# Identity products and moved weight work in the opening of a delta-rule attention and PReLU kernel

## The chip, the cores and the metric

One Trainium2 chip, one of its cores. The core has TensorE (PE: products; its weight loads are listed as PEld and run beside the products), VectorE (DVE), ScalarE (ACT), GpSimd (POOL) and SyncE (SP, which here issues nearly all DMAs). Each engine works its own queue in order. The metric is the device time of one execution in microseconds (us); lower is better. The kernel before takes 647.66 us, the median of three runs (646.80 to 648.08).

## The reference

Four batches, eight heads, 768 tokens, head dimension 48. The delta rule runs over the tokens of each head and reads each output before its own update; the outputs then go through a feed-forward layer with a PReLU whose slope `alpha` is one number per hidden unit:

```python
def _attn_ref(q, k, v, beta):
    k_n = k / (np.linalg.norm(k, axis=-1, keepdims=True) + 1e-06)
    state = np.zeros((B, H, D, D))
    for t in range(S):
        y[:, :, t] = q[:, :, t] @ state            # per batch and head
        v_old = state.T @ kt
        state = state + bt * outer(kt, vt - v_old)

def _moe_ref(x, w_in, w_out, alpha):               # x: (3072, 384)
    h = x @ w_in                                   # (384, 2048)
    g = np.maximum(h, 0.0) + alpha * np.minimum(h, 0.0)
    return g @ w_out                               # (2048, 384)
```

All data are 32-bit floats.

## The kernel before

**Tiling.** The tokens are cut into 12 chunks of 64; two batches share the 128 partitions, so there are 24 steps, numbered n, two for each chunk. Within a chunk the recurrence is a triangular system. It is solved by elimination on DVE and by small products on TensorE (48 or 64 rows, 64 columns, 32 for a step); a state per head is carried from chunk to chunk. The outputs are flipped and fed to the feed-forward products, which fill TensorE for most of the time. The engines' orders are written out by hand (`manual_schedule`): each engine works the instructions in the order of the program text, and waits only where data or a buffer make it.

**The opening** (L1691 to L1788) prepares steps 0 to 3 before the first state exists. For key n, `flipped` (L436) turns the tile on TensorE by four transposes (L430) and gives back ACT's copy out of PSUM (L439) as a piece, run by `now`. `grams` (L476) multiplies the flipped keys with themselves (32 products, L486). `squared` and `norms` make the keys' norms on ACT and DVE, `pick` and `picks` (L637, L647) gather the diagonal blocks of a gram, on ACT (L641) and DVE (L643), and `betas` (L325) flips the betas on TensorE (L330) and gives back four pieces, two on DVE and two on ACT (L338, L340), named `signs` where it is called. `first_weights` (L604) makes the weights from norms and betas on POOL. With all four grams gathered, `weigh_own` (L651) and `eliminate_small` (L666, called at L1782) solve the small blocks on DVE, and `first_chunk` (L1583, called at L1788) goes on from there: `place_small` makes the inverses on DVE (L706), `matrix` multiplies with them on TensorE (L857) and has ACT copy the product (L884), `own_values` does the same for the values with a copy on DVE (L895), `turn_values` follows on POOL (L873), and three rounds of products (L857, L912) lead to the outputs of the first chunk (L930). `query_flip` (L1553) and `queries` (L1562) do for the queries what `flipped` and `grams` do for the keys; the query products are copied by ACT (L1573).

**Fillers.** `identities` (L1549) multiplies the identity with itself; each call of `matmul` in 32-bit floats makes two products in the trace, so `identities(5)` is ten (L1551), written to the first bank of the second PSUM pair. `busy(n, p)` (L1534) multiplies the identity with `k_early[2]`: whole numbers of n make 512 columns, the rest a part of them (L1539). None of their results is read.

**Buffers.** Keys come through three tiles, `k_early[n % 3]` (L129), except key 3. Later keys take the places of earlier ones: key 6 goes to `k_early[0]`, key 5 to `k_early[2]`, key 4 to `k_early[1]`. The PSUM pairs `big[0]`, `big[1]`, `big[2]` hold the grams of steps 0, 1 (and 3), 2 in the opening.

**Weights.** `w_in` is fetched in pieces of 512 KB by `fetch_in(n)`, which issues DMAs on SP until n pieces are asked for. A piece is converted by two operations on ACT (`begin_in(n)`: L240, L242 for each piece, until n pieces are begun) and then by DVE (L256) and POOL (L263), called `convert` in `first_chunk`. In the opening, `fetch_in(1)` stands between the loads of keys 6 and 5 and that of key 4; the queries of steps 2 and 3 are loaded after that, then `fetch_in(STAGED)` brings the count to four. `pause` (L1666) has POOL write one element of a stage (L1668), so that SP's next weight loads wait for POOL's place in the order.

Of the kernel before, what the change touches and what calls it, by code (L numbers as in the profile page):

```python
# [43 lines left out]
def kernel(  # L44
# [11 lines left out]
    nc = tc.nc  # L56
# [17 lines left out]
    doubles, big, ffn_banks = ExitStack(), [], []  # L74
# [6 lines left out]
    def ps_one():  # L81
        return ps_big()[:, 0]
# [21 lines left out]
    def half(i):  # L104
        return slice(64 * i, 64 * i + 64)

    def dims(i):
        return slice(64 * i, 64 * i + D)
# [15 lines left out]
    ident = const.tile([128, 128], FP32, name="ident")  # L124
# [4 lines left out]
    def early(n):  # L129

        return k_late[1] if n == NKE else k_early[n % NKE]

    def fetch(a, n, dst, queues=(nc.sync, nc.sync)):
        c, bp = steps[n]
        for t in range(2):
            src = a[2 * bp + t, :, c * C : (c + 1) * C, :].rearrange("h p d -> p h d")
            queues[t].dma_start(out=dst[half(t)], in_=src)

    def load_early(n, *queues):
        if n < N:  # L140
            fetch(k, n, early(n)[:, :, 0:D], *queues)
# [15 lines left out]
    def load_q(n):  # L157
        if n < N:
            fetch(q, n, q_pad[n % NQ][:, :, 0:D])

    def load_v(n):
        if n < N:
            v_raw[n] = work.tile([128, H, D], FP32, name="v_raw", bufs=3)
            fetch(v, n, v_raw[n])
# [160 lines left out]
    def betas(first, last, p):  # L325
        n = last - first
        p = p[:, 0 : n * B * H].rearrange("p (c b t h) -> p c b t h", c=n, b=NB, t=2)
        for c in range(n):
            at = (first + c) * 128
            nc.tensor.transpose(  # L330
                p[:, c].rearrange("p b t h -> p (b t h)"), beta_sb[:, at : at + 128],
                ident[: B * H, : B * H],
            )
        to = beta_t.rearrange("p (c i) b h -> p i c b h", i=2)[:, :, first:last]

        def turned_sign(t, i):
            if i == 0 and first == 0:
                nc.vector.tensor_scalar_mul(to[half(t), i], p[half(i), :, :, t], -1.0)  # L338
            else:
                nc.scalar.mul(to[half(t), i], p[half(i), :, :, t], -1.0)  # L340

        return [lambda t=t, i=i: turned_sign(t, i) for t in range(2) for i in range(2)]
# [4 lines left out]
    def slopes():  # L347
        p = ffn_banks[1][:, 0:FT]
        nc.tensor.transpose(p, al_sb, ident[:FT, :FT])
        nc.scalar.activation(al_t, p, ACT.Copy, scale=-1.0, bias=1.0)  # L350
# [33 lines left out]
    def squared(n):  # L384
        ksq[n] = work.tile([128, H, D], FP32, name="ksq", bufs=2)
        nc.scalar.square(ksq[n], early(n)[:, :, 0:D])

    def norms(n):
        if n < 4:
            norm = first_norm[:, n]  # L390
        else:
            norm = stats[n] = work.tile([128, H], FP32, name="norm", bufs=EARLY + 3)
        nc.vector.tensor_reduce(out=norm, in_=ksq.pop(n), axis=AXX, op=ALU.add)
# [34 lines left out]
    def flip(src, p):  # L428
        for g in range(G):
            nc.tensor.transpose(  # L430
                p[0:ROWS, g * 128 : (g + 1) * 128],
                src[:, 2 * g : 2 * g + 2].rearrange("p h d -> p (h d)")[:, 0:ROWS],
                ident,
            )

    def flipped(n, p):  # L436
        flip(early(n), p)
        k_t[n] = work.tile([128, G, 128], FP32, name="k_t", bufs=EARLY + 1)
        return [lambda: nc.scalar.copy(k_t[n].rearrange("p g i -> p (g i)")[0:ROWS], p[0:ROWS])]  # L439
# [23 lines left out]
    def quarters():  # L463
        return [(g, a, t) for g in range(G) for a in range(2) for t in range(2)]

    def now(pieces):
        for x in pieces:
            x()
# [197 lines left out]
    def eliminate_small():  # L666

        flat = first_block[:, 0:512]

        def blocks_of(x):  # L670
            return x.rearrange("p (s b c) -> p c s b", s=2, c=LB)

        half_turns(
            flat.rearrange("p (s c r) -> p c s r", s=2, c=LB), blocks_of(first_flat[:, 0:512])
        )
        x = flat.rearrange("p (s r c) -> p s r c", s=2, c=LB)
        for j in range(1, LB - 1):
            n = LB - 1 - j
            prod = work.tile([128, HB * HB // 4], FP32, name="prod", bufs=2)
            prod = prod[:, 0 : 2 * j * n].rearrange("p (s c i) -> p s c i", s=2, c=j)  # L680
            nc.vector.tensor_tensor(
                out=prod,
                in0=x[:, :, 0:j, j : j + 1].to_broadcast([128, 2, j, n]),
                in1=x[:, :, j : j + 1, j + 1 : LB].to_broadcast([128, 2, j, n]),
                op=ALU.mult,
            )
            nc.vector.tensor_tensor(
                out=x[:, :, 0:j, j + 1 : LB], in0=x[:, :, 0:j, j + 1 : LB], in1=prod, op=ALU.add
            )
        nc.vector.memset(flat.rearrange("p (s e) -> p s e", s=2)[:, :, :: LB + 1], 1.0)  # L690
        own = work.tile([128, NJ * H, HB], FP32, name="inverse", bufs=1)
        own = own.rearrange("p b c -> p (b c)")[:, 0:512]
        half_turns(blocks_of(own), flat.rearrange("p (s c r) -> p r s c", s=2, c=LB))
        inverse[0] = own.rearrange("p (b c) -> p b c", c=LB)
# [155 lines left out]
    def heads(x):  # L850
        return x.rearrange("p (a g) i -> p a g i", a=2)
# [682 lines left out]
    def busy(n, p=None):  # L1534

        p = ps_one() if p is None else p
        while n > 0:
            x = p[:, 0 : int(512 * min(n, 1))]
            nc.tensor.matmul(  # L1539
                x, ident, k_early[2].rearrange("p h d -> p (h d)")[:, 0 : x.shape[-1]]  # L1540
            )
            n -= 1
# [3 lines left out]
        for _ in range(n):  # L1546
            nc.tensor.matmul(p[0:32, 0:32], ident[0:32, 0:32], ident[0:32, 0:32])

    def identities(n):  # L1549
        for _ in range(n):  # L1550
            nc.tensor.matmul(big[1][:, 0, 0:128], ident, ident)  # L1551

    def query_flip(n, p):  # L1553

        flip(q_pad[n % NQ], p)
        q_t[n] = beside[steps[n][1]][:, :, :, D : D + C]
        return lambda: nc.scalar.copy(
            q_t[n].rearrange("p t g i -> p g t i")[0:ROWS],
            p.rearrange("p (g t i) -> p g t i", g=G, t=2)[0:ROWS],
        )  # L1560

    def queries(p):  # L1562

        p = p.rearrange("p a (n g i) -> p a n g i", n=2, g=G)
        for n in range(2):
            for g, a, t in quarters():
                nc.tensor.matmul(
                    p[half(t ^ a), a, n, g], k_t[n][dims(a), g, half(t)],
                    q_t[n][dims(a), t, g],
                )  # L1570
            a_t[n] = work.tile([128, H, C], FP32, name="a_t")
        for n in range(2):
            nc.scalar.copy(heads(a_t[n]), p[:, :, n])  # L1573

        def mask(n):
            nc.gpsimd.tensor_tensor(
                out=a_t[n], in0=a_t[n], in1=minus[:, None, :].to_broadcast([128, H, C]),
                op=ALU.mult,
            )

        return mask
# [70 lines left out]
    n = 2 * W_IN_P  # L1652
# [9 lines left out]
    fetch_in, begin_in, conv_in = weights(pieces, stages, ids, in_done, STAGED, len(pieces))  # L1662
# [36 lines left out]
    def key(n):  # L1699
        return flipped(n, ffn_banks[n % 2])  # L1700

    def gram(n):
        return grams(n, big[n % 3 or n // 3], n // 3)

    identities(5)
    for n in (0, 2, 3):
        copy_late(n)
    squared(0)
    copy_0 = key(0)
    signs = betas(0, 1, big[2][:, 0])  # L1710
    norms(0)
    now(copy_0)
    now(signs)
    gram_0 = gram(0)
    squared(1)
    copy_1 = key(1)
    norms(1)
    pick(0, gram_0, 0)
# [7 lines left out]
    norms(2)  # L1726
    for n in (6, 5):
        load_early(n)
    fetch_in(1)
    now(copy_2)  # L1730
    gram_1 = gram(1)
    pick(1, gram_1, 0)
# [23 lines left out]
    turned_q = query_flip(0, ffn_banks[1])  # L1756
    load_q(2)
    turned_q()
    turned_q = query_flip(1, ffn_banks[0])
    load_q(3)  # L1760
    fetch_in(STAGED)
# [4 lines left out]
    nc.scalar.mul(minus, minus, -1.0)  # L1766
    for n in (2, 3):
        load_v(n)
    mask = queries(big[0])
    slopes()  # L1770
    for n, p in ((5, ffn_banks[0]), (6, big[2][:, 0])):
        now(flipped(n, p))
    busy(3.6, big[1][:, 0])
    copy_4 = flipped(4, big[2][:, 1])
    now(copy_4)
    begin_in(1)
    busy(1.0, big[1][:, 0])
    for n in (2, 3):
        query_flip(n, ffn_banks[3 - n])()
    begin_in(2)  # L1780
    busy(1.3, big[1][:, 0])
    eliminate_small()  # L1782

    def convert(n):
# [116 lines left out]
    n = WHOLE + PIECES - BEGUN - SOON  # L1901
# [28 lines left out]
    n = OUT_PARTS - few - 2 * rest + 1  # L1930
# [131 lines left out]
```

## Time and profile before

| what | before |
|---|---|
| median of three runs | 647.66 us (646.80 to 648.08) |
| the profiled execution's own time | 648.86 us |
| its span, first to last instruction | 647.1 us |
| mean granted TensorE clock | 0.995 |
| PE busy | 632.3 us, 98% of the span |
| DVE, ACT, POOL busy | 483.2, 259.4, 126.4 us |
| moved by DMA | 36.89 MB, mean 57 GB/s |

The span is what the profiler saw of the program; the execution's own time is 1.76 us longer. The page cuts the span into 40 slices of 16.2 us and gives busy shares in tenths (9 is 90% or more); PEclk is the granted TensorE clock:

```profile
PE   7889999999999999999999999999999999999997
PEld 6567787567889989989989989989999999999997
DVE  5868689978998788578678577678868568477383
ACT  6678555245553253254154144034045054042240
POOL 7188510010001000000000010000044053062360
PEclk9799999999999999999999999999999999999999
```

The first three slices hold TensorE below 90%, and the second has the only clock under 0.9. The stages at issue all lie in the first 42 us. In the other views a line reads: start, length, engine, line of the kernel, operation, what is written and from what, shapes and how many; in brackets how long the engine was idle before it, and what ended that idle time. A matmul's length includes the way through the array, so products that follow each other overlap in the list.

### The profile page before, as it was taken

The page shows a single profiled execution, that of the slowest core. Times are in us where ns is not written, and L with a number is a line of the kernel's source. Part 1 is how long each engine was busy: PE and PEld are TensorE (multiplying, and loading weights), DVE is VectorE, ACT ScalarE, POOL GpSimd, SP SyncE. Part 2 cuts the span into 40 slices and gives each one's busy share as a digit, 9 for nine tenths or more (in the row PEclk, how much of TensorE's full clock was granted, in tenths as well). Part 3 has the DMA queues.
Part 4 walks back from the last instruction along what each step waited for, and adds up shares of the span by engine and source line. Part 5 has one row for each costly group of instructions (what it writes and reads, how often), then busy time and mean ns, then how long its engine had stood idle before and what let it go on. Part 6 is the DMA issues. An engine that isn't in the chain of part 4 may idle for free.

```text
span 647.1 us, 21355 instructions
## 1 busy us (share of the span) xinstructions
PE 632.3 (98%) x9159; PEld 558.9 (86%) x9159; DVE 483.2 (75%) x1157; ACT 259.4 (40%) x605; POOL 126.4 (20%) x251
## 2 busy tenths in 40 slices
PE   7889999999999999999999999999999999999997
PEld 6567787567889989989989989989999999999997
DVE  5868689978998788578678577678868568477383
ACT  6678555245553253254154144034045054042240
POOL 7188510010001000000000010000044053062360
PEclk9799999999999999999999999999999999999999
DMA  7869753113511320321210211121220210100000
GB/s 122 201 187 223 212 135 87 22 30 63 99 27 29 75 50 2 69 39 21 59 29 15 46 32 26 38 44 21 45 43 17 54 23 2 38 3 3 24 1 26
DMA packets 106799, 36.89 MB, mean 57 GB/s; under 512 B 99872, under 2 KB 103088, under 8 KB 106704
## 3 DMA queue, kind: packets, MB, share of 16 engines
q1 hardware_dynamic: 104832, 35.03, 24.4%
q8 instruction: 72, 1.18, 0.7%
q10 hardware_dynamic: 1872, 0.49, 0.4%
q14 instruction: 23, 0.19, 0.1%
HBM read 30.78 MB, written 4.72 MB: 55 GB/s over the span
## 4 chain that ended last, share of the span: by engine, by line
PE 80%; DVE 8%; DMA 4%; ACT 3%; POOL 1%; issue 1%; SPq 1%; POOLq 0%; ACTq 0%; DVEq 0%
PE p_ffn L1075 20%; PE p_ffn L1140 17%; PE p_more L1392 8%; PE p_more L1308 5%; PE p_ffn L1118 4%; PE p_ffn L1298 3%; PE p_ffn L1392 3%; PE p_ffn L1303 2%; PE p_pair L430 2%; PE p_pair L807 2%; PE p_pair L747 2%; PE p_pair L917 2%; PE p_pair L930 2%; PE p_pair L486 1%; PE p_pair L795 1%
## 5 line engine op out<-in xcount | busy, mean ns | idle before, releaser
L1075 PE MATMUL p_ffn<-xt,w_in 128*128 128x256 f32 x768 | 177.5, 384 | 1.1 <-DVE act L1087 0.5
L1075 PEld LDWEIGHTS p_ffn<-xt,w_in 128*128 128x128 f32 x768 | 142.0, 190 | 21.9 <-issue 2.0
L1087 DVE SCALAR_TENSOR_TENSOR act<-act,al_t,p_ffn 128x256 f32<-128x256 f32 x112 | 48.5, 474 | 21.1 <-ACT act L1085 21.0
L1085 ACT ACTIVATE act<-p_ffn 128x512 f32<-128x512 f32 x56 | 33.3, 595 | 77.1 <-PE p_ffn L1075 76.8
L1332 POOL TENSOR_TENSOR k_t<-k_t 128x128 f32<-128x128 f32 (+1 forms) x48 | 29.5, 615 | 167.5 <-ACT k_t L1327 165.0
L571 DVE TENSOR_TENSOR block<-block,prod 128x30 f32<-128x30 f32 (+9 forms) x150 | 50.0, 333 | 5.2
L565 DVE TENSOR_TENSOR prod<-block 128x30 f32<-128x30 f32 (+9 forms) x150 | 49.1, 327 | 4.2 <-POOL block L555 2.7
L419 POOL TENSOR_TENSOR beta_t<-beta_t,rec 128x8 f32<-128x8 f32 x20 | 5.1, 254 | 237.5 <-DVE rec L413 221.7
L1140 PE MATMUL p_ffn<-w_out,act 128*128 128x192 f32 x288 | 49.6, 328 | 0.0
L1140 PEld LDWEIGHTS p_ffn<-w_out,act 128*128 128x128 f32 x288 | 46.5, 190 | 0.3
L973 ACT COPY xt<-p_pair 128x384 f32<-128x384 f32 x22 | 10.4, 477 | 90.6 <-PE p_pair L969 76.8
L1332 POOL TENSOR_TENSOR block<-block 128x128 f32<-128x128 f32 (+1 forms) x48 | 27.7, 576 | 16.7 <-ACT block L1327 14.2
L1298 PE MATMUL p_ffn<-xt,w_in 128*128 128x256 f32 x96 | 28.7, 381 | 0.5 <-DVE o_sb L1160 0.5
L759 ACT COPY inv<-p_pair 32x256 f32<-32x256 f32 x40 | 14.5, 362 | 24.9 <-DVE u L921 24.1
L1346 DVE SCALAR_TENSOR_TENSOR act<-block,al_t,act 128x256 f32<-128x256 f32 x32 | 19.7, 657 | 5.2 <-ACT block L1342 5.1
L1160 DVE TENSOR_TENSOR o_sb<-u,p_ffn 128x192 f32<-128x192 f32 x24 | 7.9, 351 | 20.4 <-PE p_ffn L1140 20.0
L799 ACT COPY y<-p_pair 128x384 f32<-128x384 f32 x22 | 10.5, 479 | 30.4 <-PE p_pair L795 28.8
L1327 ACT COPY k_t<-p_more 128x512 f32<-128x512 f32 x16 | 9.4, 587 | 31.4 <-PE p_more L1308 26.7
L825 DVE TENSOR_TENSOR r<-v_raw,p_pair 64x192 f32<-64x192 f32 (+1 forms) x60 | 21.2, 353 | 1.0
L1392 PE MATMUL p_more<-w_out,act 128*128 128x192 f32 x128 | 21.9, 329 | 0.0
L921 DVE TENSOR_TENSOR u<-p_pair,wgt 128x384 f32<-128x384 f32 x20 | 11.1, 556 | 14.0 <-PE p_pair L747 14.0
L807 PE MATMUL p_pair<-beside,k_t 48*64 48x112 f32 x704 | 21.4, 259 | 0.2 <-ACT beside L458 0.2
(285 smaller groups left out, 1418.0 us busy)
## 6 DMA issues: line engine op xcount, KB each, us to landing
v_raw<-in_v_dram SPq DMA_DIRECT2D x48, 96.0 KB, 2.9
qp<-in_q_dram SPq DMA_DIRECT2D x48, 96.0 KB, 2.9
out_dram<-o_sb SPq DMA_DIRECT2D x90, 48.0 KB, 1.6
space_out<-in_moe_w_out_dram SPq DMA_DIRECT2D x11, 384.0 KB, 4.0
ke<-in_k_dram SPq DMA_DIRECT2D x43, 96.0 KB, 3.1
kl<-in_k_dram SPq DMA_DIRECT2D x80, 48.0 KB, 2.6
w_out<-in_moe_w_in_dram SPq DMA_DIRECT2D x6, 512.0 KB, 4.8
w_out<-in_moe_w_out_dram SPq DMA_DIRECT2D x5, 384.0 KB, 4.9
```

The lines of the kernel that those rows point to most:

```text
L565: nc.vector.tensor_tensor(out=prod, in0=r[:, 0:j, j : j + 1].to_broadcast([128, j, n]), in1=r[:, j : j + 1, j + 1 : HB].to_broadcast([128, ...
L571: nc.vector.tensor_tensor(out=r[:, 0:j, j + 1 : HB], in0=r[:, 0:j, j + 1 : HB], in1=prod, op=ALU.add)
L807: nc.tensor.matmul(p[half(t ^ a), a, g], k_t[n][dims(a), g, half(t)], beside[bp][dims(a), t, g])
L1075: nc.tensor.matmul(p_h[:, i], w_in[:, t, (f + i) * 128 : (f + i + 1) * 128], xt[:, t], start=(t == 0), stop=(t == KT - 1),)
L1085: nc.scalar.activation(g, p_h, ACT.Relu, scale=-1.0)
L1087: nc.vector.scalar_tensor_tensor(out=g[:, i], in0=g[:, i], scalar=al_t[:, f + i : f + i + 1], in1=p_h[:, i], op0=ALU.mult, op1=ALU.add,)
L1118: nc.tensor.matmul(p_o[u], gs[f // 2][:, f % 2, u * 128 : (u + 1) * 128], w_out[:, f], start=(f == 0), stop=(f == FT - 1),)
L1140: nc.tensor.matmul(p, x(i), w(i), start=(i == 0), stop=(i == FP - 1))
L1298: nc.tensor.matmul(p[:, f * 256 : f * 256 + 256], w(2, f), xt[:, 2], start=True, stop=False)
L1308: nc.tensor.matmul(q[:, j], a, b, start=True, stop=True)
L1332: nc.gpsimd.tensor_tensor(out=dst, in0=a, in1=b, op=ALU.add)
L1392: nc.tensor.matmul(p, x(i), w(i), start=(i == 0), stop=(i == FP - 1))
```

## The change

`identities` takes the PSUM tile to write to. In the opening:

- ahead of everything six identities for five;
- one identity between the flips of key 0 and the flips of the betas;
- the signs of the betas (two operations on DVE, two on ACT) behind the first gram and the square of key 1, no longer ahead of them;
- the second piece of `w_in` is asked for together with the first, on SP ahead of the load of key 4 and of the queries of steps 2 and 3;
- three identities between the query flips of steps 0 and 1, two ahead of the query products;
- three whole `busy` products ahead of the flips of the later keys, which now come in the order 6, 5, 4; the other `busy` calls get other lengths (1.6, 0.6 and 1.0 for 3.6, 1.0 and 1.3);
- both weight pieces are begun on ACT in one go, ahead of key 4's copy; before, the first was begun behind that copy and the second behind the copies of the query flips.

```diff
-    def identities(n):
+    def identities(n, p):
         for _ in range(n):
-            nc.tensor.matmul(big[1][:, 0, 0:128], ident, ident)
+            nc.tensor.matmul(p[:, 0:128], ident, ident)
...
-    identities(5)
+    identities(6, big[1][:, 0])
     for n in (0, 2, 3):
         copy_late(n)
     squared(0)
     copy_0 = key(0)
+    identities(1, big[1][:, 0])
     signs = betas(0, 1, big[2][:, 0])
     norms(0)
     now(copy_0)
-    now(signs)
     gram_0 = gram(0)
     squared(1)
+    now(signs)
     copy_1 = key(1)
     norms(1)
...
     for n in (6, 5):
         load_early(n)
-    fetch_in(1)
+    fetch_in(2)
     now(copy_2)
...
     turned_q()
+    identities(3, big[0][:, 0])
     turned_q = query_flip(1, ffn_banks[0])
     load_q(3)
     fetch_in(STAGED)
...
     for n in (2, 3):
         load_v(n)
+    identities(2, big[0][:, 0])
     mask = queries(big[0])
     slopes()
-    for n, p in ((5, ffn_banks[0]), (6, big[2][:, 0])):
+    busy(3.0, big[2][:, 1])
+    for n, p in ((6, big[2][:, 0]), (5, ffn_banks[0])):
         now(flipped(n, p))
-    busy(3.6, big[1][:, 0])
-    copy_4 = flipped(4, big[2][:, 1])
-    now(copy_4)
-    begin_in(1)
-    busy(1.0, big[1][:, 0])
+    begin_in(2)
+    busy(1.6, big[1][:, 0])
+    now(flipped(4, big[2][:, 1]))
+    busy(0.6, big[1][:, 0])
     for n in (2, 3):
         query_flip(n, ffn_banks[3 - n])()
-    begin_in(2)
-    busy(1.3, big[1][:, 0])
+    busy(1.0, big[1][:, 0])
     eliminate_small()
```

## The prediction

> **What bounds the kernel now.** Over the whole span TensorE does: the page's chain of waits is 80% PE. The diff only touches the first 31 us, where the products wait for other engines, so I read that stretch by three views.
>
> First, busy time cut at the instants at which the granted clock changes (recorded at 10.44, 17.27 and 24.10 us, multiples of 3.41 us apart); columns are stretch, length, busy time of PE, PEld, DVE, ACT, POOL, then clock, DMA share, GB/s:
>
> ```profile
> 3.62:7.03 3.41, 2.56 (x36) 1.79 (x38) 1.49 (x8) 2.33 (x6) 2.79 (x13) 1.00 1.27 189
> 7.03:10.44 3.41, 3.41 (x55) 2.82 (x50) 2.30 (x7) 2.65 (x8) 2.53 (x9) 1.00 0.75 119
> 10.44:13.86 3.42, 2.62 (x77) 2.19 (x76) 2.63 (x9) 2.83 (x10) 2.42 (x9) 1.00 0.62 115
> 13.86:17.27 3.41, 2.09 (x71) 1.54 (x69) 3.17 (x9) 3.35 (x13) 3.14 (x8) 1.00 0.72 124
> 17.27:20.68 3.41, 2.24 (x20) 2.11 (x11) 3.03 (x12) 2.72 (x9) 0.38 (x1) 0.50 1.14 249
> 20.68:24.10 3.42, 3.42 (x6) 1.35 (x5) 3.01 (x13) 0.59 (x1) 0.00 (x0) 0.50 0.93 148
> 30.92:34.33 3.41, 2.21 (x136) 1.99 (x132) 2.65 (x5) 3.19 (x8) 3.29 (x5) 1.00 0.00 0
> ```
>
> The clock is halved at 17.27, after a stretch that TensorE filled to 2.09/3.41 = 61%, and given back at 24.10 after one filled to 100%. Ahead of 10.44 the clock column has no record, but the products tell: flips (L430) follow each other every 0.21 us before it and every 0.11 after, so the opening ran at half clock until 10.44. 75% (3.62 to 7.03) did not raise the clock, 100% did; 65% (30.92 to 34.33) kept it.
>
> Second, the chain of waits of the first 60 us (start, length, what):
>
> ```profile
> 14.88 3.77 DMA ke<-in_k_dram
> ...
> 18.78 1.07 PE p_ffn L430 x4
> 19.86 0.85 PE p_pair L430 x4
> 20.71 4.84 PE p_pair L1539 x8
> 25.55 0.45 PE p_pair L430 x4
> 26.00 0.02 issue
> 26.02 0.59 ACT k_t L439
> 26.61 0.59 ACT w_in L240
> ...
> 27.91 0.95 ACT beside L1557 x2
> 28.86 0.60 ACT w_in L240
> 29.46 0.02 issue
> 29.48 0.68 ACT w_out L242
> 30.16 0.48 ACT act L884
> ```
>
> Key 5 lands at 18.65, the flips and fillers (L1539) run at half clock to 26.0, and four weight conversions (L240, L242) stand in ACT's queue behind key 4's copy. Third, the timeline, which has what waits for that:
>
> ```profile
> 26.34 1.29 DVE L706 TENSOR_TENSOR inv<-inverse,block 128x512 f32<-128x512 f32 x2
> 28.77 0.69 PE L857 MATMUL p_pair<-inv,sums 64*64 64x64 f32 x32
> 30.05 0.56 DVE L895 COPY act<-p_pair 128x384 f32<-128x384 f32 x1 [1.40 <-PE p_pair L857]
> 30.68 0.86 POOL L873 COPY act<-act 64x192 f32<-64x192 f32 x2 [13.03 <-DVE act L895]
> ```
>
> DVE's first inverse is ready at 26.34 + 0.65 = 26.99, the matrix product that reads it starts at 28.77, its copy on ACT (L884) at 30.06, DVE's copy of the values at 30.05 after 1.40 us idle. From 30.68 POOL runs without a break but for 0.39 us until its memset at 40.95 releases the next weight loads; all later work hangs on that.
>
> **The change, step by step.** (1) Opening fillers. The sixth identity adds two products of 0.21: the ten now end at 3.83 (the last starts at 3.62), so twelve end at 4.26; key 0's flip starts at 4.33: nothing on the path. The one behind the flips adds 0.43, from 5.22 to 5.65; the betas wait for their DMA until 5.99: hidden by that DMA, 0.43 if it were early. The fill of 3.62 to 7.03 rises from 75% to some 95%, nearest to the row that raised the clock, so I take the clock at 7.03 instead of 10.44. Then key 1's flips end 0.5 us sooner, and the gram of 1 takes 0.69 us (row at 10.89) for 1.13 (row at 9.17). Behind it ACT has a root, a square and a copy (0.22, 0.51, 0.58) ahead of the pick that DVE waits for, so that this pick starts at about 9.8 instead of 10.37, and DVE's solve 0.6 us sooner. Ends: 0 (clock still at 10.44) and 0.65. The signs moved behind key 1's square let that square start at 6.35 (key landed 6.31) instead of 7.16 and end their own row at 7.5 for 7.13; POOL's first reader starts at 9.82: nothing.
>
> (2) Stands of 13.86 to 17.27. Three identities (6 products, 0.11 each) fit between the query flips at 13.96 and 14.87, as those wait for ACT's signs (0.7 idle). Two (0.43) go ahead of the query products, which start at 15.9 instead of 15.44; their ACT reader (L1573) starts at 18.17, which covers 1.0 us and more. Fill: 61% + 1.07/3.41 = 92%, so the clock stays at 17.27.
>
> (3) The new wait. busy(3.0) now stands ahead of the flips and its operand is k_early[2], the tile that key 5 is loaded into (5 mod 3 = 2). So it waits for the landing at 18.65 as the flip did, with both flips, key 4, the query flips and the matrix product queued behind it; TensorE stands from 17.6 to 18.75 as before. That stretch is filled to about 65%, between the 61% that halved the clock and the 65% that kept it; I take kept. Ends: kept, or half clock from 20.68 on (a rival below).
>
> (4) The second weight piece ahead of key 4 in SP's queue: one issue more (0.61) and 512 KB more ahead of keys 4 and queries 2 and 3. Those landed at 16.93 + 5.5 = 22.4 and 19.90 + 4.0 = 23.9. The first piece landed 1.8 us after key 5; at the 393 GB/s of 26 to 27 us it is 1.3; I take 1.5 (ends 0 and 1.8): 23.9 and 25.4. The value loads and pieces 2 and 3 come out the same, as the sum of bytes is.
>
> TensorE from 18.75 at full clock: 2.56 (six 512-wide at 0.43), 0.86 (two keys), 1.37 (busy 1.6) = 23.5; key 4 at 23.9 to 24.35; busy(0.6) to 24.9; query flips, held by 25.4, to 25.85; busy(1.0) to 26.7. The inverse is ready at 26.99 - 0.6 = 26.4, so the matrix product starts at 26.7 for 28.77: -2.05.
>
> (5) ACT: its 4.69 us idle ahead of 26.02 takes the four conversions. Copies of keys 6 and 5 to 23.15, conversions (4 x 0.69) to 25.9, key 4's copy to 26.5, two query copies (1.05) to 27.55, L884 there for 30.06: -2.5. The piece has landed by 22 (its predecessor at 15.53 + 4.9 = 20.4, plus 1.5).
>
> (6) What is late next is DVE: its three scalings (L845) ended at 28.65, now 28.05; the values product ends at 26.7 + 0.5 + 0.6 = 27.8. So L895 starts at 28.05 for 30.05: -2.0; POOL starts as much sooner and wins part of its 0.39 idle. Sum: **-2.1 us**; without step 1's 0.6, -1.4. Nothing else loads from HBM between 30.92 and 34.33 (0 GB/s), so the rest follows.
>
> That execution took 648.86 (span 647.10 and 1.76 around it): 646.8. The runs' median, 647.66, lies 1.2 under it: either profiling costs that, and the change gives 645.6, or this execution's half-clock stretch was longer than usual, which the change removes in any case, and 646.8 stands. Between them, -1.55 on the median: **646.1**.
>
> The Trainium skill (TensorE: Matmul & The Clock Gate, Why this matters for your kernels) asks only that TensorE have no idle gap above some 3 us. By that, fillers in stands of 0.7 us are for nothing, and the sum would be -1.4 at most, from step 5 and the moved flips; the trace differs, as the clock fell at 17.27 with no stand over 0.75 us since 4.33.
>
> **Rivals.** *The gate's instant.* The clock changes at fixed steps of 3.41 us that need not start with the kernel. In another execution TensorE can be given its clock back at 22 instead of 24.1: the flips then end 1.0 us sooner, and ACT's and DVE's stands shrink by as much, so the kernel before loses less. For it: 1.3 us between its fastest and slowest run. Against: key 5's wait is there in each. The change is then worth 0.6 instead of 1.55: 647.1. The same comes out if step 1 does not raise the clock early (-1.4 from 648.86, 647.5, at worst).
>
> The same skill page (Part 1: The HAM clock gate) calls this window free-running and says not to fit a cold count; no single trace here can show that.
>
> *Slower: the clock is halved later.* From 30.5 to 33.9 TensorE is filled to 59%. Two us sooner, that thin stretch meets other gate instants; if one stretch falls under the 61%, the clock is halved over the rounds. Two rounds and the outputs, 64 products each, cost 0.95 more each (twice 1.13 - 0.69, and the tail), the flips and feed-forward products behind them another 0.4: 646.1 + 3.2 = 649.3. The same price if key 5's wait costs the clock from 20.68 for two steps. Against: 65% kept it, and the stands there get shorter.
>
> **Chances.** As forecast 0.58, range 645.0 to 646.4; the gate's instant 0.28; halved later 0.14. A measurement here tells 0.2% (1.3 us) from nothing: faster than 646.36 is the first case, 0.58; same 0.28; slower 0.14. Range 645.0 to 648.0: it leaves out the slower case and a little below.
>
> **What would show it.** Right: 0.11 us between key 1's flips (step 1); granted clock 1.00 from 17 to 24 (2, 3); busy(3.0) starting at 18.7; query flips near 25.4 (4); L240 and L242 ahead of key 4's copy, L884 near 27.5 (5); L895 near 28.0 and POOL's memset near 38.9 (6). Wrong: the clock at 0.50 anywhere in 17 to 40, key 4's flip still at 25 or later, or POOL's memset at 40 with all of that in place.

## The result and the profile after

| what | before | after |
|---|---|---|
| median of the runs side by side | 648.17 us (18 runs, 646.80 to 650.24) | 650.41 us (18 runs, 648.46 to 652.65) |
| ratio, 95% interval | 1 | 1.0035 (1.0023 to 1.0047) |
| the profiled execution | 648.86 us, span 647.1 | 651.83 us, span 650.1 |
| mean granted clock in it | 0.995 | 0.997 |

The change makes the kernel 2.2 us slower; I had forecast 1.55 us faster, and the measured time lies above my range. The page of after, its first part (busy us, share, instructions) and the clock by slices, then its line of the queue that brings TensorE's own instructions (packets, MB, share of 16 engines):

```profile
PE 634.0 (98%) x9173; PEld 561.9 (86%) x9173; DVE 482.4 (74%) x1157; ACT 258.9 (40%) x605; POOL 126.6 (19%) x251
...
PEclk9989999999999999999999999999999999999999
...
q8 instruction: 72, 1.18, 0.8%
```

The dip of the clock has moved from the second slice (16 to 32 us) to the third (32 to 49 us). TensorE has 9173 products and as many weight loads for 9159: 28 instructions more, the seven added identities at two products and two loads each.

The same stretches of after, cut at the instants at which its granted clock changes (11.04, 34.93, 38.35); columns as before (busy PE, PEld, DVE, ACT, POOL; clock; DMA share; GB/s):

```profile
4.22:7.63 3.41, 3.14 (x42) 2.56 (x41) 1.15 (x5) 2.36 (x8) 2.51 (x10) 1.00 1.36 185
7.63:11.04 3.41, 3.41 (x43) 2.94 (x43) 2.46 (x8) 2.48 (x7) 2.75 (x11) 1.00 0.66 116
14.45:17.86 3.41, 3.10 (x79) 2.58 (x77) 3.14 (x8) 3.37 (x12) 3.14 (x6) 1.00 0.77 146
17.86:21.27 3.41, 2.71 (x7) 1.25 (x8) 3.01 (x12) 1.66 (x6) 0.00 (x0) 1.00 1.03 307
...
31.51:34.93 3.42, 1.59 (x76) 1.25 (x67) 1.62 (x5) 3.17 (x8) 3.34 (x4) 1.00 0.02 5
34.93:38.35 3.42, 3.30 (x117) 3.30 (x121) 1.99 (x5) 1.16 (x2) 2.16 (x3) 0.50 0.38 93
```

The opening keeps its clock from 11.04 on, as the change meant it to. The rounds lose it: 31.51 to 34.93 is filled to 1.59/3.42 = 47%, and the next stretch runs at half clock.

The chain of waits of after (start, length, what) in the stretch where before had the flips at half clock and ACT's conversions:

```profile
22.26 1.57 SPq L137
23.83 0.05 issue
23.88 3.65 DMA qp<-in_q_dram
27.53 0.14 issue
27.66 0.62 PE p_ffn L430 x4
```

The conversions are off the chain; in their place stands the load of query 3, issued by SP at 23.83 and landed at 27.53. The timeline from there on (idle before in brackets, with what ended it):

```profile
29.07 0.69 PE L857 MATMUL p_pair<-inv,sums 64*64 64x64 f32 x32
30.36 0.56 DVE L895 COPY act<-p_pair 128x384 f32<-128x384 f32 x1 [1.55 <-PE p_pair L857]
30.98 0.85 POOL L873 COPY act<-act 64x192 f32<-64x192 f32 x2 [13.20 <-DVE act L895]
...
32.00 0.67 PE L857 MATMUL p_pair<-act 64*64 64x48 f32 x29 [0.34 <-DVE act L895]
34.03 0.78 PE L857 MATMUL p_pair<-act 64*64 64x48 f32 x35 [1.37 <-issue]
35.94 2.00 PE L857 MATMUL p_pair<-r,act 64*64 64x48 f32 x64
38.98 1.30 POOL L263 TENSOR_TENSOR w_in<-w_out,w_in 128x512 uint32<-128x512 uint32 x1 [1.88 <-DVE w_out L256]
42.96 0.09 POOL L1668 MEMSET space_out<- 1x1 f32 x1
```

and of before, the lines of its rounds, which were not shown:

```profile
33.71 1.15 PE L857 MATMUL p_pair<-act 64*64 64x48 f32 x64 [0.83 <-DVE act L912]
35.07 1.15 PE L857 MATMUL p_pair<-r,act 64*64 64x48 f32 x64 [0.21 <-DVE r L912]
36.52 0.40 PE L930 MATMUL p_pair<-u,a_t 64*64 64x48 f32 x10 [0.30 <-DVE u L912]
37.26 1.30 POOL L263 TENSOR_TENSOR w_in<-w_out,w_in 128x512 uint32<-128x512 uint32 x1 [0.39 <-DVE w_out L256]
37.38 1.02 PE L930 MATMUL p_pair<-u,a_t 64*64 64x48 f32 x54 [0.47 <-issue]
```

Up to L873 the two are 0.30 us apart (30.98 and 30.68). The loss is made behind it. In the first round, 29 products into step 1, TensorE stops from 32.45 to 34.03 and waits for "issue", which is nothing that any engine or data DMA releases. Then the third round runs at half clock, 2.00 us for 1.15. DVE's conversion (L256) stands behind the last round's operation in DVE's queue, POOL's L263, which waits for it, starts 1.72 us later than before, and POOL's memset comes at 42.96 for 40.95: 2.0 of the 3.0 us by which the two spans differ. The other 1.0 arises later; I did not follow it.

### The profile page after: what moved, and what is told of

Same layout as the page of the kernel before. It is cut to its first block, busy times and chain, and to the rows that moved or that the text cites. A ratio compares the mean times of both kernels' runs of the same rounds, so it can differ in the third digit from the quotient of the medians.

```text
span 650.1 us, 21384 instructions
## 1 busy us (share of the span) xinstructions
PE 634.0 (98%) x9173; PEld 561.9 (86%) x9173; DVE 482.4 (74%) x1157; ACT 258.9 (40%) x605; POOL 126.6 (19%) x251
## 3 DMA queue, kind: packets, MB, share of 16 engines
q8 instruction: 72, 1.18, 0.8%
## 4 chain that ended last, share of the span: by engine, by line
PE 86%; DVE 6%; ACT 2%; DMA 2%; issue 2%; POOL 1%; SPq 0%; POOLq 0%; DVEq 0%; ACTq 0%
PE p_ffn L1075 24%; PE p_ffn L1140 17%; PE p_more L1392 8%; PE p_more L1308 5%; PE p_ffn L1118 4%; PE p_ffn L1298 3%; PE p_ffn L1392 3%; PE p_ffn L1303 2%; PE p_pair L430 2%; PE p_pair L807 2%; PE p_pair L747 2%; PE p_pair L486 2%; PE p_pair L930 2%; PE p_pair L917 2%; PE p_pair L795 1%
## 5 line engine op out<-in xcount | busy, mean ns | idle before, releaser
L1327 ACT COPY k_t<-p_more 128x512 f32<-128x512 f32 x16 | 9.4, 586 | 31.6 <-PE p_more L1308 27.9
```

## What TensorE waits for: its own instructions

Before also stops twice for "issue": at 37.38, ten products into the outputs, and at 42.31. I counted TensorE's records (products, weight loads and the few others) up to each such stop: they come behind record 961, 1217 or 1473, 256 apart, in every kernel of this study, whatever the work there (in e7_192_more and e10_wide_weights_back behind record 705 too). The page's line for queue 8, of kind "instruction", fits: 72 packets and 1.18 MB are 16.4 KB each, and before's 18,448 records (9159 products, as many weight loads, 130 others) over as many packets are 256 each; the two kernels with 192 instructions more have 73 packets. So TensorE's instructions come in blocks of 256, and a **block end** is a place where it has to have the next one.

The trace's records of queue 8 show when a block is fetched. In the stretch at issue, from record 449 to 1217, it is in every kernel here behind the first instruction of the block before it; elsewhere in the span it is often ahead of it, by up to 5.5 us. In the table, the start of the block ahead (record 705), the fetch that follows, and the first instruction behind record 961:

| kernel | record 705 | fetch | behind 961 | stood for it since |
|---|---|---|---|---|
| before | 29.88 | 30.67 to 31.63 | 33.88 | not at all; waited for DVE until 33.71 |
| after | 29.96 | 31.67 to 32.82 | 34.03 | 32.45 |
| e5_wide_identities | 28.25 | 30.62 to 31.85 | 33.11 | 31.23 |
| e11_no_identities | 29.14 | 29.96 to 31.11 | 32.39 | 32.12 |
| e9_values_held | 29.00 | 29.75 to 30.71 | 31.94 | not at all |
| e7_192_more | 20.41, next at 22.17 | 28.49 to 29.92 | 31.29 | 30.00 |

Where TensorE stands waiting, it goes on 1.2 to 1.4 us after the fetch has ended; from record 705 that is 3.3 to 4.9 us in all (9.1 in e7_192_more from 22.17, as it stood at record 705 itself until then). A round of 64 products is 128 instructions, or two rounds a block, for which TensorE has 2.3 us of work at full clock. So matrix, values, rounds and outputs together use up blocks about as fast as they can come. Each added instruction ahead shifts every block end towards earlier work, and that is what the later experiments turn on: **28 more instructions move the end at 961 from product 11 of the second round to product 29 of 32 in the first round's step 1, and the end at 1217 from product 10 of the outputs to the last few products of the third round.**

## The experiments

Each kernel was timed in five rounds beside the kernel before (12 runs, but 11 of e11, 7 of e4, and 6 of e7 and e9; 29 or 30 runs of the kernel before in each group). The row of after is the result above, 18 runs of each. "More" counts TensorE's instructions against before, ahead of the first chunk.

| kernel | more | block end 961 falls in | ratio (95%) | fastest run, us | POOL's memset, us |
|---|---|---|---|---|---|
| e2_weights_only | 0 | round 2 | 0.9994 (0.9981 to 1.0008) | 647.29 | 39.36 |
| e5_wide_identities | 0 | round 2 | 1.0003 (0.9982 to 1.0024) | 647.12 | 39.97 |
| e10_wide_weights_back | 0 | round 2 | 1.0004 (0.9992 to 1.0015) | 647.40 | 41.59 |
| e11_no_identities | 0 | round 2 | 1.0009 (0.9998 to 1.0021) | 647.57 | 40.66 |
| e15_wide_28_behind | 0 (28 behind) | round 2 | 1.0010 (0.9993 to 1.0027) | 646.55 | 40.13 |
| e13_wide_16_more | 16 | round 2, its start | 1.0002 (0.9989 to 1.0015) | 647.35 | 40.56 |
| after | 28 | round 1, step 1 | 1.0035 (1.0023 to 1.0047) | 648.46 | 42.96 |
| e1_weights_back | 28 | round 1, step 1 | 1.0034 (1.0019 to 1.0048) | 648.84 | 41.22 |
| e3_identities_only | 28 | round 1, step 1 | 1.0028 (1.0017 to 1.0039) | 648.36 | 41.79 |
| e4_second_begun_late | 28 | round 1, step 1 | 1.0054 (1.0031 to 1.0077) | 650.42 | 42.61 |
| e6_28_more | 28 | round 1, step 1 | 1.0020 (1.0003 to 1.0037) | 648.72 | 41.62 |
| e12_wide_28_more | 28 | round 1, step 1 | 1.0029 (1.0019 to 1.0039) | 648.37 | 41.75 |
| e14_wide_48_more | 48 | round 1, step 1 | 1.0031 (1.0016 to 1.0046) | 649.18 | 41.97 |
| e8_weights_192_more | 192 | values | 1.0033 (1.0012 to 1.0053) | 648.93 | 40.72 |
| e7_192_more | 220 | matrix of step 1 | 1.0092 (1.0060 to 1.0124) | 652.65 | 44.84 |
| e9_values_held | 0 | round 2 | 1.0055 (1.0038 to 1.0071) | 650.62 | 44.15 |

The memset's time is that of one profiled execution each, and this need not be a typical one: it lies above the kernel's median by 1.4 us in after and e3, 2.1 in e5, 2.8 in e13 and 3.2 in e10 (which stood 2.06 us at record 705 besides), and below it by 1.2 in e2 and 2.0 in e1. So a profile shows where TensorE stops; what that costs is read from the ratios.

### The parts of the change apart

**e1_weights_back** is the changed kernel with the weight work where it was:

```diff
-    fetch_in(2)
+    fetch_in(1)
...
-    begin_in(2)
     busy(1.6, big[1][:, 0])
     now(flipped(4, big[2][:, 1]))
+    begin_in(1)
     busy(0.6, big[1][:, 0])
     for n in (2, 3):
         query_flip(n, ffn_banks[3 - n])()
+    begin_in(2)
```

> The changed kernel with the weight work put back as it was before (one piece fetched ahead of key 4, the first begun behind key 4's copy, the second behind the query copies); all fillers, the order of the keys and the signs stay changed. Queue theory (the second piece on SP ahead of key 4 and the queries holds up query 3, which landed at 27.5 us, and with it the matrix product at 29.07): query 3 lands near 24 again, the matrix product starts at 26.5 to 27.2, and the time is 1.5 to 2.5 us under the changed kernel's, a ratio to before of 0.997 to 1.000. Gate theory (the loss is the half clock over the rounds, 34.9 to 38.4 us, wherever the matrix product starts): a half-clock stretch between 28 and 38 again, and a ratio of 1.002 to 1.004 in spite of the earlier product. Filler theory (products added to the opening delay it): the ratio stays at 1.003.

**e2_weights_only** is the kernel before with the weight move alone (`fetch_in(2)` ahead of key 4, one `begin_in(2)` ahead of its filler).

> The kernel before with the weight work alone moved: two pieces fetched ahead of key 4, both begun on ACT ahead of key 4's copy; no filler and no order of keys changed. Queue theory: query 3 lands near 27.5, the matrix product starts at 29.2 to 29.6 for 28.77, ratio 1.001 to 1.004. Gate and filler theories: the clock and the products are those of before, ACT is freed by 1.4 us ahead of its matrix copy: ratio 0.997 to 1.000.

**e3_identities_only** is the kernel before with the added identities and the moved signs, and nothing else of the change.

> The kernel before with the identities and the place of the signs changed alone; weights, busy products and the order of the keys as before. Queue theory: clock kept at 17.3 where it fell, so the flips and fillers run at full clock and the matrix product starts at 26.5 to 27.5 for 28.77: ratio 0.997 to 0.999. Gate theory: a half-clock stretch later, between 28 and 40, ratio 1.000 to 1.003. Filler theory: 1.002 to 1.004.

**e4_second_begun_late** is e1_weights_back without its last `begin_in(2)`; the second piece is then begun by the first chunk's own conversions.

> As the first of these runs, but ACT begins the second piece only where its conversion on DVE asks for it, behind the first chunk's matrix copies, instead of behind the query copies. Queue theory: ACT's matrix copy starts right behind the product, near 27.6 instead of 28.9, ratio 0.995 to 0.999, at most that of the first run. Gate theory: 1.001 to 1.004 with a half-clock stretch in the rounds. Filler theory: 1.003.

The second weight piece ahead of the queries was my first suspect, as query 3 landed so late in after. It fell: the move alone gives 0.9994, and without it the loss is all there (1.0034). The identities alone bring it (1.0028). e3_identities_only is telling beyond its ratio: its matrix product starts at 26.64 and L895 at 28.24, 1.8 us sooner than in before, and it is slower all the same. Its timeline of TensorE:

```profile
30.00 0.67 PE L857 MATMUL p_pair<-act 64*64 64x48 f32 x29 [0.38 <-DVE act L895]
32.90 2.13 PE L857 MATMUL p_pair<-act 64*64 64x48 f32 x67 [2.24 <-issue]
```

TensorE reaches the same product, the 29th of step 1, 2.0 us sooner than in after, and then stands 2.24 us there. e4_second_begun_late stops at it as well (2.12 us for "issue"); why it is slower than e1_weights_back, if it is (the intervals overlap), I did not pursue.

### Fill or number of instructions

**e5_wide_identities** has all of the change, but identities up to four abreast, so that the same columns take 20 instructions, as the five of before did, for 48:

```diff
     def identities(n, p):
-        for _ in range(n):
-            nc.tensor.matmul(p[:, 0:128], ident, ident)
+        while n > 0:
+            m = min(n, 4)
+            nc.tensor.matmul(
+                p[:, 0 : 128 * m].rearrange("p (r e) -> p r e", r=m), ident,
+                ident[:, None, :].to_broadcast([128, m, 128]),
+            )
+            n -= m
```

> The changed kernel with its identity products made up to four times as wide (512 columns), so that TensorE streams the same columns in as many instructions as the kernel before. Block theory (TensorE's instructions come in blocks of 256; the 28 added ones put the end of a block behind product 29 of the rounds' 64, where TensorE stands 0.5 to 2.2 us for the next block, and that stand costs it the clock): the stand is found at product 11 of the following 64 as in the kernel before and in the run with the weights alone, under 1 us, no half clock in the rounds, ratio 0.998 to 1.001. Gate theory (it is the fill that the identities add, which saves the clock at 17 us and loses it in the rounds): ratio 1.002 to 1.005 as before. Queue theory is out by the first four runs.

**e6_28_more** is the kernel before with 28 of the shortest instructions (seven products of 32 x 32, two each, with their loads) ahead of key 5's flip:

```diff
+    short(7, ffn_banks[0])
```

> The kernel before with seven products of 32x32 (28 instructions, some 0.4 us) in TensorE's stand at 17.5 us and nothing else. They add no fill to speak of. Block theory: the stand at product 29 of a round appears, the ratio is 1.001 to 1.004 and the executions fall in two groups some 2 us apart. Gate theory: ratio 0.999 to 1.001.

**e10_wide_weights_back** is e1_weights_back with wide identities; **e11_no_identities** is the changed kernel with the identities and the signs as before; **e12_wide_28_more** is e5_wide_identities with the line of e6_28_more ahead of key 6's filler.

> e1_weights_back (the weight work as before the change) with identity products up to 512 columns wide, so that TensorE has as many instructions as before the change. Instruction blocks: the stand at record 961 falls on the product that had it before the change, and the ratio comes down from 1.0034 to 0.996 to 1.000. Clock gate: the same fill as in e1_weights_back and so the same time, 1.002 to 1.005.

> The changed kernel with the identity products and the place of the signs as before the change: what is left of the change is the fillers ahead of the flips and the weight move. Instruction blocks: the count is that of before, 0.997 to 1.001. Fillers or weight move as the cause: 1.002 to 1.005, as the change as a whole.

> e5_wide_identities and 28 short instructions of TensorE ahead of key 6's filler, so that the count is that of the changed kernel while the identity products stay wide. Instruction blocks: the loss comes back, 1.002 to 1.005, and the stand at record 961 falls early in the rounds. Clock gate and fillers: as e5_wide_identities, 0.998 to 1.001.

The number decides, not the fill. With the same fill and 28 instructions fewer, the loss goes from 1.0035 to 1.0003 and from 1.0034 to 1.0004; put back as 28 instructions of no use, it returns (1.0029); given to the kernel before, they cost 0.20%. The pair e1 and e10 is the clearest, as its intervals lie apart (from 1.0019 up, and up to 1.0015); those of after and e5 just touch. In e6 TensorE's timeline shows the end at record 1217 inside the third round:

```profile
34.56 1.14 PE L857 MATMUL p_pair<-r,act 64*64 64x48 f32 x61 [0.21 <-DVE r L912]
36.31 0.32 PE L857 MATMUL p_pair<-r,act 64*64 64x48 f32 x3 [0.61 <-issue]
```

The two intervals with wide identities do not reach down to 0.9976, the 1.55 us of the forecast, so the gain that I hoped for did not appear either. For the place of the stops, e5 and e12 make the cleanest pair, since they start the first chunk alike. The timeline of e12_wide_28_more:

```profile
27.21 0.69 PE L857 MATMUL p_pair<-inv,sums 64*64 64x64 f32 x32
28.75 0.56 DVE L895 COPY act<-p_pair 128x384 f32<-128x384 f32 x1
...
30.26 0.67 PE L857 MATMUL p_pair<-act 64*64 64x48 f32 x29 [0.22 <-DVE act L895]
32.85 0.78 PE L857 MATMUL p_pair<-act 64*64 64x48 f32 x35 [1.92 <-issue]
37.76 1.30 POOL L263 TENSOR_TENSOR w_in<-w_out,w_in 128x512 uint32<-128x512 uint32 x1 [2.35 <-DVE w_out L256]
41.75 0.09 POOL L1673 MEMSET space_out<- 1x1 f32 x1
```

and of e5_wide_identities:

```profile
27.14 0.69 PE L857 MATMUL p_pair<-inv,sums 64*64 64x64 f32 x32
28.74 0.56 DVE L895 COPY act<-p_pair 128x384 f32<-128x384 f32 x1
...
30.25 1.19 PE L857 MATMUL p_pair<-act 64*64 64x48 f32 x43 [0.22 <-DVE act L895]
33.11 1.02 PE L857 MATMUL p_pair<-act 64*64 64x48 f32 x53 [1.67 <-issue]
37.00 1.30 POOL L263 TENSOR_TENSOR w_in<-w_out,w_in 128x512 uint32<-128x512 uint32 x1 [1.59 <-DVE w_out L256]
37.18 1.74 PE L930 MATMUL p_pair<-u,a_t 64*64 64x48 f32 x54 [0.67 <-issue]
39.97 0.09 POOL L1673 MEMSET space_out<- 1x1 f32 x1
```

L895 starts at 28.75 and 28.74. They then stand 2.1 and 1.9 us behind record 961; what differs is the place: within round 1 (29 of 32 products of step 1) or within round 2 (32 of round 1 and 11 more). In e5 both of DVE's operations on round 1 are done by 31.61, ahead of the stand's end; in e12 the second starts at 33.26 only. POOL's L263 follows at 37.76 and 37.00, the memset at 41.75 and 39.97. (The whole execution of e5's profile was no shorter for it, 650.97 us for 650.47: it ran at half clock from 34.7 to 44.9, e12's from 34.5 to 37.9. The medians are 648.85 and 650.23.) That raised the question of the last group of runs.

### Number or place

**e13_wide_16_more** and **e14_wide_48_more** are e12_wide_28_more with `short(4, ...)` and `short(12, ...)`. **e15_wide_28_behind** has the 28 instructions behind the first chunk's outputs:

```diff
-        to_ffn(0, ps_ffn())
+        p = ps_ffn()
+        short(7, p)
+        to_ffn(0, p)
```

> e5_wide_identities and 16 short instructions ahead of key 6's filler (28 in e12_wide_28_more). By the place of the block ends, the end at record 1217 comes 2 products into the first chunk's outputs (10 in e5_wide_identities, and 4 products ahead of the last round's end with 28), so the stand there is behind the last round again and the loss is gone: 0.998 to 1.0015. If short instructions cost by their number alone, 16/28 of 0.29%: 1.0017, from 1.0007 to 1.0025.

> e5_wide_identities and 48 short instructions ahead of key 6's filler. By the place of the block ends, the end at record 1217 comes 14 products ahead of the last round's end, and the loss is that of 28: 1.002 to 1.0045. If short instructions cost by their number alone, 48/28 of 0.29%: 1.005.

> e5_wide_identities and 28 short instructions behind the first chunk's outputs (ahead of the flips for the feed-forward products, where TensorE waits for DVE's copy), so that only block ends from record 1473 on move. By the place of the block ends: no loss, 0.998 to 1.0015. If 28 more instructions cost wherever they stand: 1.002 to 1.004.

The place fits all three results, the number alone does not. 16 instructions show no cost (1.0002, up to 1.0015), 28 cost 0.29%, and 48 cost no more than 28 (1.0031, up to 1.0046, for the 1.005 that the number would give). The run with 16 does not tell the two readings apart by itself, since the number alone would allow 1.0007 to 1.0025. TensorE's timeline of e13_wide_16_more:

```profile
30.66 1.07 PE L857 MATMUL p_pair<-act 64*64 64x48 f32 x35 [0.22 <-DVE act L895]
33.11 1.14 PE L857 MATMUL p_pair<-act 64*64 64x48 f32 x61 [1.39 <-issue]
...
36.12 0.42 PE L930 MATMUL p_pair<-u,a_t 64*64 64x48 f32 x2
36.90 1.95 PE L930 MATMUL p_pair<-u,a_t 64*64 64x48 f32 x62 [0.36 <-issue]
```

and of e14_wide_48_more:

```profile
30.97 0.52 PE L857 MATMUL p_pair<-act 64*64 64x48 f32 x19 [0.35 <-DVE act L895]
33.00 2.45 PE L857 MATMUL p_pair<-act 64*64 64x48 f32 x77 [1.51 <-issue]
```

With 16 the stops come three products into round 2 (x35 is 32 and 3) and two into the outputs: the round ahead is done, and DVE and what follows it can go on while TensorE stands. With 48 the first stop is 19 products into round 1's step 1 and DVE's operation on that step waits with it. The result of e15 (1.0010, 0.9993 to 1.0027) leans the same way, and its memset is at 40.13, but its interval does not exclude 0.2%. Both block ends move together in all these kernels, so how much of the loss belongs to the end at 961 and how much to the one at 1217 stays open.

### Two misses

**e7_192_more** (e4_second_begun_late with three grams of step 0 written once more, 192 instructions, behind `slopes()`) and **e8_weights_192_more** (e2_weights_only with the same) were to move the block ends far enough that the rounds would have their instructions in time (e8, as the kernel before, without the 28):

```diff
+    for _ in range(3):
+        grams(0, big[2])
```

> The run with the second piece begun late, and the gram of key 0 made three times more ahead of the flips of keys 6 and 5 (96 products, 192 instructions, some 1.4 us in a stand of 1.2). Their results aren't read. Block theory: the block that ended at record 961 is asked for near 18 us instead of 27.4 and is there in time; no stand of over 0.5 us at record 961, the clock stays at 1.00 in the rounds, ratio 0.995 to 0.999 for 1.0054. Gate theory: fill at 17 us is higher still, and the clock is lost in the rounds as without them: ratio 1.003 to 1.006.

> The run with the weight work alone, and the gram of key 0 made three times more at the same place. Block theory: as in the run above, ratio 0.995 to 0.999. Gate theory: 0.999 to 1.003, as the added products keep the clock at 17 us and it is lost later.

**e9_values_held** is e5_wide_identities with the loads of values 2 and 3 issued behind the first chunk's `pause`, to free the queues for the fetch.

> e5_wide_identities with the loads of value steps 2 and 3 issued in the first chunk, behind POOL's wait for the stages, instead of in the opening. Instruction blocks: if a block's fetch waits behind the data loads that stand in the queues, the block that begins at record 961 is fetched within 1.2 us of record 705 (2.4 us in e5_wide_identities) and TensorE stands there for less than 1 us; the time is 0.996 to 1.000 of before, unless the later values hold up the rounds. If the fetch has its own pace whatever the loads, 705 to 961 stays at 4.9 us and the time at 0.999 to 1.002. Clock gate and fillers alone: no change from e5_wide_identities.

Both of the former were slower (1.0092 and 1.0033). In e8_weights_192_more TensorE stands 1.41 us at record 961, among the values, and 2.92 us at record 1473, which is now within the outputs (until 40.81). Its memset is not late (40.72), so its loss lies behind that. In e7_192_more TensorE reaches record 705 at 20.41 and goes on at 22.17, but the next block is fetched at 28.49 only. The DMA view of that stretch, 20.4 to 28.4 (packets, MB, share of 16 engines):

```profile
q1 hardware_dynamic: 2785, 2.01, 96.3%
```

The fetch came 6.3 us after the block ahead was entered, while query, value and weight loads kept the DMA engines full: my account lacked that an instruction fetch can be held up by data loads. e9 fits that: its fetch begins 0.75 us behind record 705 (2.37 in e5_wide_identities) and TensorE does not stand at 961. Its rounds are over 1.7 us sooner than in e5 (L930's second part at 35.46 for 37.18; part of that is e5's half clock from 34.7), but the values now come late and POOL's memset with them, at 44.15. The ratio is 1.0055. So the stand at 961 can be taken away, at a higher price in this form. No kernel here beat the kernel before.

## Why the prediction was wrong, by its steps

**Step 1, wrong in the profiled execution.** I took the clock as raised at 7.03 because a 95% fill is "nearest to the row that raised the clock". It came at 11.04: 4.22 to 7.63 is filled to 3.14/3.41 = 92% and did not raise it, 7.63 to 11.04 at 100% did; key 1's eight flips take 1.95 us, at half clock. The fallback that I had priced (0.6 us less) applies: DVE's scalings (L845) end at 28.81 for 28.65 before, and I had 28.05.

**Steps 2 and 3, right.** The stretch ahead of 17.86 is filled to 3.10/3.41 = 91% (I said 92%), and the clock stays. busy(3.0) waits for key 5 and starts at 18.56 (I said 18.7), with the clock at 1.00; its stretch is filled to 2.71/3.41 = 79% (I said 65%).

**Step 4, mis-sized in that execution.** I gave the second weight piece 1.5 us, with query 3 at 25.4. It landed at 27.53, 3.6 us later than in before: the third of SP's four query issues alone took 3.77 us (20.06 to 23.83), and the next could begin only then. So the matrix product started at 29.07, not 26.7. In e5 and e12, with the same loads, query 3's flip is at 25.69 and 25.80 and the matrix product at 27.14 and 27.21, close to what I had. The price of that wait varies between executions; it is not the cause of the loss, as e2 shows.

**Step 5, right** for the conversions: L240 and L242 run at 22.80 to 25.73, ahead of key 4's copy. L884 came at 29.84 for my 27.55 since the matrix product held it; in e12 it is at 27.97.

**Step 6 is where the prediction failed**, at "Nothing else loads from HBM between 30.92 and 34.33 (0 GB/s), so the rest follows". That the end hangs on the memset fits only roughly: span less memset is 606 to 608 us in before, in after and in all other kernels but three (609 in e5_wide_identities and e13_wide_16_more, which spent 10.2 us at half clock in their profiled executions, and 611 in e8_weights_192_more), and these 2 us are as much as the loss itself. The failure comes ahead of it: what is saved ahead of L895 does not reach the memset. e12_wide_28_more has the opening nearly as I forecast it, with L895 at 28.75 (I said 28.05) for 30.05, and is 0.29% slower. Something does load in that stretch: block by block, TensorE's instructions. In before the block fetched from 30.67 to 31.63 should have been usable at about 33.0 (an estimate, by the 1.2 to 1.4 us that TensorE needs after a fetch where it stands), and was hidden behind a DVE wait that ended at 33.71. I read that wait as DVE's, and did not ask what would be late next once it went. The term missing from my sum is the 28 added instructions in a stretch that TensorE's instruction supply bounds: steps 1 and 2 ("nothing on the path" and "covers 1.0 us and more") priced them by their time on TensorE only. And POOL's idle of 0.39 us, which I counted as something to win, was the sign that POOL's chain hangs on the rounds: what ends it is DVE's L256, which stands behind the last round, and it grew to 1.88 us in after and 2.35 in e12.

The Trainium skill (Runtime: NRT & Kernel Launch, Instruction fetch mechanics) says that instructions are refilled in blocks of 16 KiB, 256 instructions, over a DMA queue of the engine's own while the block ahead is worked off, and that this is mostly hidden. The traces agree on block and queue; they differ on hidden, with stands of up to 2.2 us at record 961 here.

**The rivals.** The clock did get halved later (34.93 to 38.35), in the slower rival's place. Its reason was another: the thin stretch, filled to 47%, holds the stand for instructions, and was not my 59% stretch at other instants of the gate. And half clock by itself does not tell the kernels apart. e5_wide_identities and e13_wide_16_more ran at half clock from 34.7 to 44.9 in their profiled executions, which were long ones, and their medians are those of before. The mean granted clock of every single run is known too: among the runs at 0.997 or more, at most one stretch of 3.41 us at half clock, after has a median of 651.2 us (5 runs) and before, in the groups of the experiments, 648.1 (29 runs); at 0.994 to 0.996 the medians are 650.4 (8) and 648.3 (54). So the loss is there at the same clock. Where in a run the clock was halved is known for the profiled executions alone, so how much of the loss a half clock in the rounds adds to the stands stays open. The gate's instant, the rival of less gain, is not what happened either.

What remains of the gain when the 28 instructions are taken out, none or up to 0.2%, these runs do not settle: e5's interval reaches down to 0.9982, and 1.0 us of the 1.3 that L895 gained was still there at the memset of its profile. e11_no_identities shows one place where it ends: it reaches record 1473 1.3 us sooner than before (40.40 for 41.71) and stands there until 42.37, the instant of before (42.31).

## What to carry to other kernels

Count a filler in instructions as well as in time: where small products follow each other closely, TensorE's instructions come in blocks, which here took 3 to 5 us to arrive and longer under heavy loads, and each instruction added anywhere ahead shifts where TensorE will stop for the next. Make fillers few and wide (here 20 instructions for 48 did the same fill with no loss that shows), and look at which side of a dependency a block end falls. Before counting on time saved early to reach the end, look in the stage behind it for idle time put down to "issue" and for waits that have been hiding it.

## What the hardware showed that I had not expected

- An instruction fetch can come late under data loads: it began 0.75 us after the block ahead was entered in e9_values_held, 2.4 in e5_wide_identities, and 6.3 us in e7_192_more, with the data queue on 96% of the engines' time. In e10_wide_weights_back the block behind record 705 was fetched 10.8 us after the one ahead of it was entered (17.1 to 27.9), and TensorE stood there.
- A DMA issue on SP, some 0.6 us as a rule, took 3.77 us in after, where the DMA share of the stretch is 1.03.
- The granted clock fell after stretches of 3.41 us filled to 47% (after), 27% (e3_identities_only, 29.74 to 33.15) and 54% (e11_no_identities, 14.77 to 18.18). It was not raised by 92%, and was by 100%. The Trainium skill (TensorE: Matmul & The Clock Gate, Why this matters for your kernels) warns of idle gaps above some 3 us only; in after the clock fell with one stand of 1.6 us and shorter ones about it.
